# A four-layer attention kernel whose weights are split into f16 pairs at fixed powers of two, with the column maxima moved into the guard

## The chip, the cores and the metric

The kernel runs on one core of one Trainium2 chip. The metric is the device time of one execution in microseconds, here the median of three runs. Beside it stands one profiled execution, from which every duration is read.

## What is computed

The reference applies four layers to x of 2048 rows and 512 columns in f32. Layers 0 and 2 attend over a sliding window of 256 positions with the weights A; layers 1 and 3 attend over all 2048 positions with the weights B. There are 32 heads of 16 columns.

```python
def layer(x, wqkv, wo, window):
    h = layernorm(x)                            # eps 1e-5, no gain
    q, k, v = split_heads(h @ wqkv)             # 32 heads of 16
    s = (q @ k.T) * 16 ** -0.5                  # window: 0 <= i - j < 256, else -1e9
    return x + (softmax(s) @ v) @ wo

x = A_x                                         # B_x is not used
for _ in range(2):
    x = layer(x, A_wqkv, A_wo, True)
    x = layer(x, B_wqkv, B_wo, False)
```

The entries of x and of all weights are drawn from a normal distribution with a spread of 0.05.

## The kernel before

There are two paths. The fast path computes everything and also a flag, `okay`, which is good when all softmax sums lie in a safe range. A general path follows under a condition and runs only where the flag isn't good.

The fast path works on chunks of 512 rows (four chunks, `c`) and on groups of four heads (eight groups, `qd`). Chunks are normalised (`stats`, `norm`), transposed by DMA into `xc` and projected by `keys`, `queries` and `values`; `wo` is the output projection (`wo_part` in layer 3), and `epilogue` divides by the softmax sums. `exps` makes scores on PE (L724) and their exponentials on ACT (L728), which `attn_win` masks on POOL (L791, L794); the sums of products with V are L801 in window layers and L768 in full ones.

A projection is exact enough through f16 pairs: a weight matrix is split into a high and a low f16 part, x too, and three of the four products are added up in PSUM (`TERMS`). For the split the columns are first scaled by powers of two taken from the column maxima. This is the preparation of a matrix: `load_w` loads the raw f32 matrix (1 MB), `maxima` reduces absolute maxima on DVE (L295) and finishes them with four transposes on PE (L300), `scales` makes the powers of two and broadcasts them over all partitions by f32 matmuls (L328), and `parts` scales the matrix (L345, on POOL for the five matrices that are prepared during layer 0), casts the high part on ACT (L346), subtracts for the low part on POOL (L347) and writes the pair to DRAM (`wd`), from which the projections load it again. The scales are undone at the evictions of the projections (`es`, L534, L536, L537) and in the output projections (`gcol`, L662 and L683, followed by an addition to x, L663 and L684).

In the opening, before layer 0's attention, chunk 0 is projected from the raw weights by f32 matmuls with a transposed f32 x (`xT`); the maxima of these three matrices are made by transposing them on PE (`first_maxima`, L310). The pairs of these matrices are made at the end of the opening and used from chunk 1 on.

The order on PE is written out by the program: a planner (`Side`) puts pieces of projections between the steps of the attention, by costs and due times on a clock of its own. Works marked `aside` (normalisation, transposes, preparation) get their pieces at every step. The order on the other engines and on the one DMA queue, SP, is made by the scheduler from the dependencies and its own estimate of times; an instruction of low priority is taken where an earlier one isn't ready yet. All transfers are issued in order on SP, so one that waits holds those behind it.

At the end of each window layer stands a tail: the output projection of chunk 3, its normalisation and the projections that need it, before the next layer can begin (the calls of `tails`). Full layers use a single PSUM bank, `acc[1]`, for all side work.

Of the kernel before, what the change touches and what calls it, by code (L numbers as in the profile page):

```python
# [36 lines left out]
L_SUM = 2.0 ** 60  # L37

# [149 lines left out]
def fast_path(ctx, tc, flag, a_x, a_wqkv, a_wo, b_wqkv, b_wo, out):  # L188
# [21 lines left out]
    CM, DN, DC, WT, ST, pend = {}, {}, {}, {}, {}, []  # L210
# [16 lines left out]
    perm = cp.tile([P, P], F32, name="perm")  # L227
    onesf = cp.tile([P, P], F32, name="onesf")
    ones = cp.tile([P, QC], F16, name="ones")
    hsum = cp.tile([P, 32], BF16, name="hsum")  # L230
    es = cp.tile([P, 2, 2, NHT], F32, name="es")
    upv = cp.tile([P, 2, NHT], F32, name="upv")
    gcol = [cp.tile([P, D], F32, name=f"gcol{i}") for i in range(2)]
# [12 lines left out]
    nc.gpsimd.tensor_copy(perm.rearrange("p (h u d) -> p u h d", u=2, d=DH), ident.rearrange("p (u h d) -> p u h d", u=2, d=DH))  # L246
# [38 lines left out]
    def maxima(ty, s, raw):  # L285

        n = f"{ty}_{s}"
        if s == 3:
            for k in range(NC):
                nc.vector.tensor_scalar(raw[:, k, :], raw[:, k, :], upv[:, ty, k:k + 1], None, op0=ALU.mult)  # L290
        cm = CM[ty, s] = vp.tile([P, NHT], F32, name=f"wc{n}", tag="wc", bufs=8)
        am = vp.tile([P, D], F32, name=f"wa{n}", tag="dn", bufs=2)
        for h in range(4):
# [3 lines left out]
            yield  # L297
        pt = bank().rearrange("p (t f) -> p t f", f=P)
        for t in range(NHT):
            nc.tensor.transpose(pt[:, t, :], am[:, t * P:(t + 1) * P], ident)  # L300
        nc.vector.tensor_reduce(cm, pt, axis=AX.X, op=ALU.max)

    def first_maxima(s, raw, tiles):

        if (0, s) not in CM:
            CM[0, s] = vp.tile([P, NHT], F32, name=f"wc0_{s}", tag="wc", bufs=8)
        for t in tiles:
            pt = bank()
            for k in range(NC):
                nc.tensor.transpose(pt[:, k * P:(k + 1) * P], raw[:, k, t * P:(t + 1) * P], ident)  # L310
            nc.vector.tensor_reduce(CM[0, s][:, t:t + 1], pt, axis=AX.X, op=ALU.max, apply_absolute_value=True)

    def scales(ty, s):

        n = f"{ty}_{s}"
        cm = CM.pop((ty, s))
        up = es[:, ty, s, :] if s < 2 else vp.tile([P, NHT], F32, name=f"wu{n}", tag="wc", bufs=8)
        dn = vp.tile([P, NHT], F32, name=f"wn{n}", tag="wc", bufs=8)
        nc.vector.tensor_scalar(up.bitcast(I32), cm.bitcast(I32), 0x7F800000, None, op0=ALU.bitwise_and)
        nc.vector.tensor_scalar(dn.bitcast(I32), up.bitcast(I32), -1, 0x7F000000, op0=ALU.mult, op1=ALU.add)  # L320
        DC[ty, s] = dn
        for v, name in ((up, "u"), (dn, "d"))[0 if s == 3 else 1:]:
            dg = vp.tile([P, NHT, P], F32, name=f"{name}g{n}", tag="oe")
            nc.vector.tensor_tensor(dg, ident[:, None, :].broadcast_to([P, NHT, P]),
                                    v[:, :, None].broadcast_to([P, NHT, P]), ALU.mult)
            yield
            pb = bank()
            nc.tensor.matmul(pb, onesf, dg.rearrange("p t f -> p (t f)"), start=True, stop=True)  # L328
            if name == "u":
                nc.vector.tensor_copy(gcol[ty], pb)  # L330
            else:
                DN[ty, s] = vp.tile([P, D], F32, name=f"wd{n}", tag="dn", bufs=2)
                nc.scalar.activation(DN[ty, s], pb, AF.Copy)
        if s == 2:
            yield
            pu = bank()
            nc.tensor.matmul(pu[:, :NHT], perm, up, start=True, stop=True)
            nc.vector.tensor_copy(upv[:, ty, :], pu[:, :NHT])

    def parts(ty, s, raw, act):  # L340

        dnb = DN.pop((ty, s))
        w = wp.tile([P, NC, 2, D], F16, name=f"w{ty}_{s}", tag="vf", bufs=NQ)
        hi, lo = w[:, :, 0, :], w[:, :, 1, :]
        mul = lambda k: (nc.vector if act else nc.gpsimd).tensor_tensor(raw[:, k, :], raw[:, k, :], dnb, ALU.mult)  # L345
        cast = lambda k: nc.scalar.activation(hi[:, k, :], raw[:, k, :], AF.Copy)  # L346
        rest = lambda k: nc.gpsimd.tensor_tensor(lo[:, k, :], raw[:, k, :], hi[:, k, :], ALU.subtract)  # L347
        if act:
            for k in range(NC):
                mul(k), cast(k), rest(k)  # L350
                yield
            WT[ty, s] = w
# [869 lines left out]
```

## Time and the profile before

| What | us |
|---|---|
| median of three runs | 2755.56 (2751.47 to 2759.08) |
| profiled execution, its own time | 2751.01 |
| its span | 2749.2 |
| first scores of layer 0 | 64.12 |
| first scores of layer 1 | 499.95 |
| last addition to x | ends at 2742.19 |

The page gives busy time by engine, and views of the trace give the same by stage. PE's busy time is modelled to the end of each matmul, and matmuls overlap. The chain of waits follows the work back from the last instruction.

### The profile page before, as it was taken

The numbers are of one execution on the slowest core, as the hardware profiler recorded it, in microseconds if no ns is written. First come the engines' busy times: TensorE is split into PE (matmuls) and PEld (weight loads), VectorE is DVE, ScalarE is ACT, GpSimd is POOL, SyncE is SP. The second block draws the span as 40 slices with busy tenths as digits, with TensorE's granted clock in tenths as the row PEclk, the third lists the DMA queues.
The fourth block names the chain that finished last, engine by engine and source line by source line (L and its number), as shares of the span: only waits on it lengthen the run. The fifth ranks groups of instructions, "written<-read, shape, count | busy, mean of one in ns | idle before, by whom it ended". The sixth has DMA issues, their size and how long they took to land.

```text
span 2749.2 us, 59656 instructions
## 1 busy us (share of the span) xinstructions
PE 2632.0 (96%) x24358; PEld 772.6 (28%) x24358; DVE 955.6 (35%) x2059; ACT 2380.7 (87%) x2687; POOL 570.4 (21%) x1129
## 2 busy tenths in 40 slices
PE   8889999999999999999999989899999999999997
PEld 4333344322222222222223333522222222222221
DVE  7678765112131113112216467411222222222222
ACT  3566664799999999999997667499999999999997
POOL 2477672000000000000006678100000000000000
PEclk9999999999999999999999999999999999999999
DMA  6877676322232123212325556622334443333321
GB/s 214 231 248 228 197 228 191 117 70 90 86 100 87 61 85 108 82 64 91 99 72 151 173 152 173 181 75 93 112 111 126 123 117 105 99 111 114 99 95 56
DMA packets 318269, 344.78 MB, mean 125 GB/s; under 512 B 114080, under 2 KB 234144, under 8 KB 311968
## 3 DMA queue, kind: packets, MB, share of 16 engines
q1 hardware_dynamic: 317984, 340.86, 41.1%
q8 instruction: 193, 3.16, 0.5%
q14 instruction: 92, 0.75, 0.1%
HBM read 228.07 MB, written 96.99 MB: 118 GB/s over the span
## 4 chain that ended last, share of the span: by engine, by line
PE 74%; DVE 8%; ACT 7%; issue 4%; DMA 3%; POOL 2%; SPq 1%; ACTq 0%; DVEq 0%; POOLq 0%
PE acc L768 31%; PE s L724 19%; PE acc L435 10%; PE b L438 9%; ACT e L728 7%; PE acc L801 4%; PE bs L438 1%; DVE ot L696 1%; DVE sp L537 1%; POOL wr L345 1%; DVE xh L477 1%; DMA qt<-qs 1%; DVE xn L471 1%; DVE xh L471 1%; POOL e L791 0%
## 5 line engine op out<-in xcount | busy, mean ns | idle before, releaser
L728 ACT ACTIVATE e<-s 128x1024 f32<-128x1024 f32 (+2 forms) x2432 | 2246.5, 1114 | 122.4 <-PE s L724 107.3
L768 PE MATMUL acc<-e,vt 128*17 128x512 f32 x8192 | 1080.8, 599 | 5.2 <-DVE ot L696 4.2
L724 PE MATMUL s<-qt,kt 64*128 64x512 f16 (+3 forms) x5504 | 772.3, 355 | 52.4 <-ACT e L728 26.6
L724 PEld LDWEIGHTS <-kt 64*128 64x128 f16 x5504 | 199.6, 94 | 798.7 <-issue 765.9
L794 POOL TENSOR_SCALAR_AFFINE_SELECT e<-e 128x256 f32<-128x256 f32 x512 | 229.8, 457 | 106.6 <-ACT e L728 106.3
L768 PEld LDWEIGHTS acc<-e,vt 128*17 128x17 f32 x8192 | 136.3, 95 | 385.4 <-issue 353.1
L696 DVE STREAM_TRANSPOSE ot<-acc 128x512 f32<-128x512 f32 x128 | 91.4, 714 | 410.5 <-PE acc L768 320.7
L791 POOL TENSOR_SCALAR_AFFINE_SELECT e<-e 128x256 f32<-128x256 f32 x448 | 203.0, 459 | 81.7 <-ACT e L728 77.9
L712 POOL TENSOR_TENSOR oh<-o,oh 128x512 f16<-128x512 f32 x31 | 36.0, 1162 | 881.4 <-DVE oh L711 881.4
L801 PE MATMUL acc<-e,vt 128*17 128x384 f32 (+2 forms) x2816 | 202.1, 393 | 4.1 <-POOL e L791 4.0
L438 PE MATMUL b<-xc,w 128*128 128x512 f16 x672 | 159.6, 385 | 11.9 <-DVE sp L537 7.8
L542 POOL TENSOR_TENSOR sq_h<-sp_h 128x512 bf16<-128x512 f16 x27 | 28.1, 1041 | 486.3 <-DVE sp_h L536 486.3
L536 DVE TENSOR_SCALAR sp<-acc,es 128x512 f16<-128x512 f32 x28 | 20.9, 747 | 288.9 <-PE acc L435 277.1
L536 DVE TENSOR_SCALAR sp_h<-acc,es 128x512 f16<-128x512 f32 x27 | 20.3, 750 | 283.4 <-PE acc L435 283.3
L542 POOL TENSOR_TENSOR sq<-sp 128x512 bf16<-128x512 f16 x28 | 29.1, 1041 | 396.8 <-DVE sp L536 396.8
L648 DVE COPY vt<-acc 128x256 f32<-128x256 f32 (+1 forms) x36 | 18.5, 514 | 265.5 <-PE acc L435 265.5
L435 PE MATMUL acc<-xc,w_h 128*32 128x512 f16 x1296 | 108.5, 379 | 2.3 <-DVE km L575 2.3
L435 PE MATMUL acc<-xc,w 128*32 128x512 f16 x1344 | 108.9, 379 | 0.3
L683 DVE TENSOR_TENSOR dx<-acc,gcol 128x512 f32<-128x512 f32 x60 | 41.5, 692 | 176.6 <-PE acc L435 176.6
L435 PE MATMUL acc<-wo,oh 128*32 128x512 f16 x1296 | 101.4, 379 | 0.0
L534 ACT ACTIVATE sp<-b,es 128x512 f16<-128x512 f32 x56 | 38.5, 687 | 71.1 <-PE b L438 71.0
L438 PEld LDWEIGHTS <-w 128*128 128x128 f16 x720 | 66.5, 99 | 110.2 <-issue 42.2
(172 smaller groups left out, 1807.2 us busy)
## 6 DMA issues: line engine op xcount, KB each, us to landing
kt<-kf SPq DMA_DIRECT2D x128, 512.0 KB
qt<-qs SPq DMA_DIRECT2D x128, 256.0 KB
xd<-x SPq DMA_DIRECT2D x96, 256.0 KB
x<-xd SPq DMA_DIRECT2D x96, 256.0 KB
w<-wd SPq DMA_DIRECT2D x20, 1024.0 KB
kt<-kw SPq DMA_DIRECT2D x64, 256.0 KB
qs<-sp SPq DMA_DIRECT2D x48, 256.0 KB
wo<-wd SPq DMA_DIRECT2D x12, 1024.0 KB
```

The source lines that it names most:

```text
L435: nc.tensor.matmul(ps[g:g + 32], a[:, g:g + 32], b, start=(i == 0), stop=(i == len(pairs) - 1), skip_group_check=True)
L438: nc.tensor.matmul(ps, a, b, start=(i == 0), stop=(i == len(pairs) - 1))
L471: norm1 = lambda o: nc.vector.tensor_scalar(o, xs[i], mv[:, i, 0:1], y[:, i:i + 1], op0=ALU.subtract, op1=ALU.mult)
L542: nc.gpsimd.tensor_tensor(sq, sp[:, 0], sp[:, 0], ALU.mult)
L683: nc.vector.tensor_tensor(d, ps, gcol[1], ALU.mult)
L696: nc.vector.transpose(ot.rearrange("p b r -> p (b r)"), a)
L724: nc.tensor.matmul(ps[:, h, s0:s0 + wd_], kt[R * h:R * h + R, pr, kc:kc + P], qt[R * h:R * h + R, pr, qc:qc + wd_], start=True, stop=True)
L728: nc.scalar.activation(e[:, :, w0:w1], ps[:, :, w0:w1], AF.Exp, scale=SCALE)
L768: nc.tensor.matmul(a[32 * h:32 * h + DH + 1, :], V[l, qd // 4, j // 8][:, j % 8, 4 * (qd % 4) + h, :], es_[h // 2][:, h % 2, :], start=(j ...
L791: nc.gpsimd.affine_select(v, v, pattern=[[0, 2], [-1, P]], compare_op=ALU.is_gt, fill=0.0, base=0, channel_multiplier=1)
L794: nc.gpsimd.affine_select(v, v, pattern=[[0, 2], [1, P]], compare_op=ALU.is_ge, fill=0.0, base=0, channel_multiplier=-1)
L801: nc.tensor.matmul(a[32 * h:32 * h + DH + 1, q * P:(q + nb) * P], V[l, (4 * c + j) // 4][:, j % 4, 4 * qd + h, :], es_[h // 2][:, h % 2, s ...
```

## The change

Every matrix is split at one fixed power of two (2^7, for V's matrix 2^5) in place of a power per column. The preparation is then a load, a cast with a scale on ACT and one operation on DVE that scales and subtracts, four of each for a matrix. The maxima, scales, broadcasts and the scaling on POOL are gone. Chunk 0 is projected from the split weights with a split x, with the product of the high parts of all four tiles first. Query, key and value matrices of type A stay in SBUF for chunks 0 and 1. The output projections use one DVE operation with a constant instead of a product with `gcol` and an addition.

The guard is extended: `column_maxima` loads each of the eight raw matrices again, in the buffers of the window layers' V, and reduces it on DVE in four pieces; these works are put beside the first half of layer 1's chunk 0. `column_range`, in layer 2, checks that all column maxima lie between 2^-8 and 3.9, and the flag includes that.

```diff
+UP = {0: 2.0 ** 7, 1: 2.0 ** 7, 2: 2.0 ** 5, 3: 2.0 ** 7}
+C_MIN, C_MAX = 2.0 ** -8, 3.9
...
-    def load_w(ty, s):
-        raw = wp.tile([P, NC, D], F32, name=f"wr{ty}_{s}", tag="vf", bufs=NQ)
+    def load_w(ty, s, tag="vf", n="wr"):
+        raw = wp.tile([P, NC, D], F32, name=f"{n}{ty}_{s}", tag=tag, bufs=VB if tag == "vw" else NQ)
...
-    def maxima(ty, s, raw):
-    def first_maxima(s, raw, tiles):
-    def scales(ty, s):
-    def parts(ty, s, raw, act):
...
+    def parts(ty, s, raw):
+        w = wp.tile([P, NC, 2, D], F16, name=f"w{ty}_{s}", tag="vf", bufs=NQ)
+        for k in range(NC):
+            nc.scalar.activation(w[:, k, 0, :], raw[:, k, :], AF.Copy, scale=UP[s])
+            nc.vector.scalar_tensor_tensor(w[:, k, 1, :], raw[:, k, :], UP[s], w[:, k, 0, :], op0=ALU.mult, op1=ALU.subtract)
+            yield
+        nc.sync.dma_start(wd[ty, s], w)
+        if ty == 0 and s < 3:
+            WT[ty, s] = [w, w]
+
+    def prep(ty, s):
+        raw = load_w(ty, s)
+        yield wait(14)
+        for _ in parts(ty, s, raw):
+            yield wait(1.8)
+
+    def column_maxima(ty, s):
+        raw = load_w(ty, s, "vw", "wq")
+        yield wait(14)
+        am = vp.tile([P, D], F32, name=f"wa{ty}_{s}", tag="am", bufs=1)
         for h in range(4):
             f = slice(h * P, (h + 1) * P)
             nc.vector.tensor_reduce(am[:, f], raw[:, :, f].rearrange("p k f -> p f k"), axis=AX.X, op=ALU.max,
                                     apply_absolute_value=True)
+            yield wait(2)
+        at = vp.tile([P, D // 32, 32], F32, name=f"wb{ty}_{s}", tag="at", bufs=1)
+        nc.vector.transpose(at.rearrange("p b r -> p (b r)"), am)
+        yield wait(1)
+        nc.vector.tensor_reduce(cmax[:, ty, s, :], at, axis=AX.X, op=ALU.max)
+        yield wait(1)
+
+    def column_range():
+        pt = bank()
+        nc.tensor.transpose(pt[:, :P], cmax.rearrange("p t s b -> p (t s b)"), ident)
+        cols = vp.tile([P, 32], F32, name="cols", tag="cols", bufs=1)
+        nc.vector.tensor_reduce(cols, pt[:, :P].rearrange("p (a r) -> p r a", r=32), axis=AX.X, op=ALU.max)
+        nc.vector.tensor_reduce(okay[:, 2:3], cols, axis=AX.X, op=ALU.min)
+        nc.vector.tensor_reduce(okay[:, 3:4], cols, axis=AX.X, op=ALU.max)
...
+        if first:
+            for t in range(NHT):
+                begun.append(bank())
+                for k in range(NC):
+                    nc.tensor.matmul(begun[t], w[:, k, 0, t * P:(t + 1) * P], xc[:, 0, k, :], start=(k == 0), stop=False)
...
-            e = first[2][:, t:t + 1] if first else es[:, ty, s, t:t + 1]
+            e = 1.0 / UP[s]
...
-                nc.vector.tensor_tensor(d, ps, gcol[l % 2], ALU.mult)
-            nc.vector.tensor_add(xs[i], xs[i], d)
+                nc.vector.scalar_tensor_tensor(xs[i], ps, 1.0 / (UP[2] * UP[3]), xs[i], op0=ALU.mult, op1=ALU.add)
...
-            nc.vector.tensor_tensor(d, ps, gcol[1], ALU.mult)
-            (nc.gpsimd if last and i % 2 == 0 else nc.vector).tensor_tensor(xs[i], xs[i], d, ALU.add)
+            nc.vector.scalar_tensor_tensor(xs[i], ps, 1.0 / (UP[2] * UP[3]), xs[i], op0=ALU.mult, op1=ALU.add)
...
-    xT = wp.tile([P, NC, QC], F32, name="xT", tag="xc", bufs=NQ)
-    first_maxima(1, raw[1], (0, 1))
+    xT = XC[0, 0] = wp.tile([P, 2, NC, QC], F16, name="xc0_0", tag="xc", bufs=NQ)
+    raw = {m: load_w(0, m, "xc") for m in (1, 0, 2)}
...
-        nc.scalar.activation(xT[:, :, i * P:(i + 1) * P], pt, AF.Copy)
+        xh, xl = (xT[:, b, :, i * P:(i + 1) * P] for b in range(2))
+        nc.scalar.activation(xh, pt, AF.Copy)
+        nc.vector.tensor_tensor(xl, pt, xh, ALU.subtract)
+    run(parts(0, 1, raw[1]))
+    run(keys(0, 0, True, None, True))
+    run(parts(0, 0, raw[0]))
+    run(queries(0, 0, True))
+    run(parts(0, 2, raw[2]))
+    vals = values(0, 0, True)
+    next(vals), next(vals), next(vals)
     settle()
...
+            return [Work(column_range(), 0.0, None, [("C", *m) for m in mats], aside=True), OO(1, 3), Q(2, 2), T(2, 3)]
...
+    for i, m in enumerate(mats):
+        works[1][0].append(CM(*m, [("C", *list(mats)[i - 2])] if i > 1 else []))
...
+    nc.vector.tensor_mul(okay[:, 0:1], okay[:, 0:1], okay[:, 2:3])
```

More of the change, by code (lines that the diff above doesn't have):

```diff
@@ L313, in scales @@
-    def scales(ty, s):
[L315 to L338, printed above, removed]
@@ L437, in mms @@
             else:
[L438 removed]
+                nc.tensor.matmul(ps, a, b, start=(go and i == 0), stop=(i == len(pairs) - 1))
             spent(us)
@@ L611, in key_shift, with values @@
                               m[32 * t:32 * t + 8, None, :].broadcast_to([8, NT, P]))
-    def values(l, c, act, first=None, halves=(0, 1), tiles=range(4)):
+    def values(l, c, act, halves=(0, 1), tiles=range(4)):
         n = f"{l}_{c}_{halves[0]}_{tiles[0]}"
         HH, D0, D1 = H // 2, halves[0] * D // 2, (halves[-1] + 1) * D // 2
-        if not first:
-            w = weights(l % 2, 2, f"v{n}", D0, D1)
-            yield wait(8)
-            xc = XC[l, c]
+        here = (l % 2, 2) in WT
+        w = weights(l % 2, 2, f"v{n}", D0, D1)
+        yield wait(0 if here else 8)
+        xc = XC[l, c]
         dst = {}
```

159 lines of the change are left out of this document (33 added, 126 removed).

## The prediction

> **What bounds the kernel now.** I read the page's busy times first, then the busy time by stage, then the chain of waits inside the stage that the change touches most; the order of instructions of the built program, which holds no times, tells where the moved work now stands. The page shows PE and ACT as the two loaded engines, but as an average over stages with different limits:
>
> ```profile
> PE 2632.0 (96%) x24358; PEld 772.6 (28%) x24358; DVE 955.6 (35%) x2059; ACT 2380.7 (87%) x2687; POOL 570.4 (21%) x1129
> ```
>
> ```profile
> 0.00:64.00 64.00, 54.64 (x176) 28.87 (x176) 48.61 (x117) 20.73 (x33) 14.09 (x24) 1.00 0.65 207
> 64.00:440.00 376.00, 342.88 (x2981) 138.92 (x2984) 260.31 (x529) 241.78 (x317) 251.56 (x527) 0.99 0.76 225
> 440.00:504.00 64.00, 58.09 (x340) 29.29 (x336) 27.70 (x59) 22.39 (x40) 1.91 (x6) 0.98 0.68 209
> 504.00:1452.00 948.00, 938.40 (x9184) 221.80 (x9186) 183.82 (x425) 942.94 (x1020) 47.55 (x46) 1.00 0.27 82
> 1452.00:1782.00 330.00, 300.14 (x2933) 125.42 (x2925) 207.16 (x474) 212.22 (x261) 206.92 (x483) 0.97 0.60 173
> 1782.00:2750.00 968.00, 937.82 (x8761) 228.34 (x8757) 228.04 (x456) 940.61 (x1020) 48.41 (x44) 0.99 0.33 102
> ```
>
> The next view splits that. Its columns are stage, length, then busy time of PE, PEld, DVE, ACT and POOL, the granted clock, the DMA share and GB/s. The rows are the opening, layer 0, its tail, layer 1, layer 2 with its tail, and layer 3. Layers 1 and 3 are bound by ACT (942.94 of 948): the change takes no ACT work out of them, so they can lose but hardly gain. Whatever comes back must come out of the first 504 us. There PE is busy 342.88 of 376, so layer 0 yields its PE work that disappears and part of 33 us of gaps. The chain through 64 to 440 says what fills them:
>
> ```profile
> by line: PE b L438 32.0%; PE acc L801 12.9%; PE s L724 6.0%; POOL wr L345 5.1%; issue 3.4%; ACT e L728 2.9%; DMA kt<-kw 2.7%; POOL e L791 2.5%; POOL e L794 2.0%; DVE xn L471 1.9%; DVE xh L477 1.8%; DVE st L457 1.7%; DVE xh L471 1.7%; DMA x<
> ```
>
> POOL's scaling of weights (L345) carries 5.1% of 376, 19 us, more than the masks (L791, L794) that queue behind it.
>
> **The opening: -12.** Two pieces of the chain that are DMAs (the load of 1 MB of raw weights, and a transposed write of x), then the timeline of the opening:
>
> ```profile
> 2.68 6.35 DMA wr<-in_A_wqkv_dram
> 1759.61 3.29 DMA xc<-xh
> ```
>
> ```profile
> 9.16 1.09 PE L310 MATMUL bs<-ident,wr 128*128 128x128 f32 x4 [9.16 <-DMA wr<-in_A_wqkv_dram]
> 9.47 1.91 DVE L1081 TENSOR_SCALAR x<-x,mv,y 128x512 f32<-128x512 f32 x4
> 14.29 0.60 ACT L1085 ACTIVATE xT<-b 128x512 f32<-128x512 f32 x1
> 17.07 3.70 PE L438 MATMUL bs<-xT,wr 128*128 128x512 f32 x8 [0.20 <-DVE wc L311]
> 43.22 0.66 DVE L457 BATCH_NORM_STATS2 st<-x 128x6 f32<-128x512 f32 x1
> 52.93 4.06 SPq L498 DMA_TRANSPOSE xc<-xh  x3
> 55.51 0.74 DVE L591 TENSOR_SCALAR m_None<-b,kx 128x512 f16<-128x512 f32 x1
> 64.12 0.50 PE L724 MATMUL s<-qt,kt 64*128 64x384 f16 x4
> 72.57 2.76 PE L438 MATMUL b<-xc,w 128*128 128x512 f16 x12
> ```
>
> Before, twelve f32 tiles at some 3.5 us make K, Q and V of chunk 0, with 12 groups of L310 transposes ahead. Now 144 f16 matmuls do it, 2.76 us for 12, nearer 2.6 in a row: 12 x 2.6 = 31 us. The first weights land at 9.16; then ACT has 4 casts of weights and 4 of x, 8 x 0.6 = 5 us, so PE starts near 14 and ends near 46. DVE, by the order, has 15 splits of x and of weights ahead of the first eviction; at 0.75 (row L537 below) that is 11.2 us after 11.4, so 22.6, in time for the fifth tile, which needs the first tile's bank near 25. The query squares come after 10 of 12 tiles, at 41; from the mask row's start (55.51) to the first scores (64.12) was 8.6, so scores start near 50, 14 earlier. What is late next is chunk 1: its x loads now stand on SP behind the queries' writes, so its statistics end near 45. They ended at 43.88 before and the last transpose was issued by 56.99; 13.1 later plus 3.29 to land gives 61. K of chunk 1 started at 72.57, so 12 remain. Bounds: 16 (x in time) and 9.
>
> **Layer 0: -15.** Groups of instructions between 64 and 440 us (count, busy time, mean ns of one, idle time before), and below them two rows of the waits between 130 and 440:
>
> ```profile
> L537 DVE SCALAR_TENSOR_TENSOR sp<-b,es,sp 128x512 f16<-128x512 f32 x40 | 29.6, 745 | 54.1 <-ACT sp L534 46.0 <-DMA kf<-sp 4.5 <-DMA kt<-kw 3.5
> L347 POOL TENSOR_TENSOR w<-wr,w 128x512 f16<-128x512 f32 x24 | 29.5, 1251 | 1.5 <-ACT w L346 1.5
> L345 POOL TENSOR_TENSOR wr<-wr,wd 128x512 f32<-128x512 f32 x20 | 27.4, 1396 | 1.1 <-ACT wd L333 1.0
> L696 DVE STREAM_TRANSPOSE ot<-acc 128x512 f32<-128x512 f32 x31 | 22.0, 711 | 22.0 <-PE acc L801 21.2
> L295 DVE TENSOR_REDUCE wa<-wr 128x128 f32<-128x512 f32 x20 | 20.3, 1067 | 2.5 <-DMA wr<-in_B_wqkv_dram 2.4
> L663 DVE TENSOR_TENSOR x<-x,dx 128x512 f32<-128x512 f32 x12 | 8.8, 737 | 0.3
> L346 ACT ACTIVATE w<-wr 128x512 f16<-128x512 f32 x24 | 14.5, 634 | 11.9 <-POOL wr L345 8.5 <-DVE wr L345 3.4
> L328 PE MATMUL b<-dg,onesf 128*128 128x512 f32 x10 | 5.6, 645 | 1.8 <-DVE dg L324 1.8
> L328 PE MATMUL b<-ug,onesf 128*128 128x512 f32 x4 | 2.2, 644 | 0.0
> L300 PE MATMUL b<-ident,wa 128*128 128x128 f32 x20 | 3.3, 287 | 0.0
> ```
>
> ```profile
> PEld acc L801 <- POOL e L791: 9.9, 18, 1.8
> PE acc L801 <- POOL e L791: 3.7, 5, 1.4
> ```
>
> The scale broadcasts (L328) and the transposes of maxima (L300) go: PE loses 5.6 + 2.2 + 3.3 = 11 us, which counts in full where PE is busy nine tenths. POOL loses 29.5 + 27.4 = 57; PE's waits for masks are 9.9 + 3.7 = 13.6, and I credit under half, 6, because a mask also waits for its exp. ACT keeps its 20 casts (0.634 each), but in fours: 2 us for exps held behind 2.5 us. DVE trades 20 reductions for 20 splits of 0.75. Together -15. Bounds: -5 (ACT lumps and DVE collisions eat the rest), -26 (11, 13.6 and some scaling stalls).
>
> A split reads two SBUF tensors while POOL masks. An old DVE op of that kind (two SBUF inputs) ran beside POOL in the opening, by the timeline:
>
> ```profile
> 36.91 5.86 POOL L347 TENSOR_TENSOR w<-wr,w 128x512 f16<-128x512 f32 x4 [33.26 <-ACT w L346]
> 39.00 1.64 DVE L345 TENSOR_TENSOR wr<-wr,wd 128x512 f32<-128x512 f32 x1
> ```
>
> It took 1.64. 20 splits at 1.64 instead of 0.75 add 18 us of DVE time; with half of that on PE's evictions, layer 0 gains 6, not 15. I take 0.75, since a mask is far shorter than POOL's weight ops. The Trainium skill, GPSIMD Engine Reference, section Specifications, says the same against this change: POOL's SBUF interface is shared with VectorE and collides with its instructions that read two SBUF inputs; by that rule the layer gains 6, and the row just shown agrees.
>
> **The column maxima: +3, +6, +1.** The diff puts them beside layer 1, but the order of instructions in the built program has seven of eight matrices' reductions on DVE ahead of layer 1: three within chunk 3, one at its end, three in the tail between the layers; only the last stands inside layer 1. In chunk 3 that is 12 x 1.067 + 3 x 0.71 = 15 us of DVE, in gaps while PE works; the second and third load wait on SP for the reductions before, with query and key loads behind: +3 (0 to 12). The tail's timeline:
>
> ```profile
> 457.80 0.32 SPq L399 DMA_DIRECT2D w<-wd  x1
> 460.20 0.17 DVE L43 TENSOR_SCALAR v<-mv 128x4 f32<-128x4 f32 x1
> 462.58 0.16 DVE L466 SCALAR_TENSOR_TENSOR nb<-mv,y 128x4 f32<-128x4 f32 x1
> 474.96 2.75 PE L438 MATMUL b<-xc,w 128*128 128x512 f16 x12 [1.09 <-DMA xc<-xh]
> ```
>
> The tail has no slack: DVE's steps from 460.20 to 462.58 lead to xc, for which PE already waits 1.09. Four reductions and a transpose now stand among those steps, 4 x 1.067 + 0.71 = 5.0 us; the query weights' load (457.80) falls behind the last x write and two column loads: +6 (0 to 13). Nothing covers either, so this is the term whose bound I trust least. In layer 1 the last matrix's four reductions wait for their load and hold an eviction of the values behind them; PE runs two or three exps ahead there, so of 5 us I take +1 (0 to 5).
>
> **The rest: -4.** One DVE op replaces product and addition (0.737 each) in the output projections. In layer 2 three stand on the chain, -2.2, and the range check (one transpose, six DVE ops) gives back 1; its tail -0.7. In layer 3 ACT hides them: 0. At the end,
>
> ```profile
> 2738.06 0.81 PE L438 MATMUL b<-wo,oh 128*128 128x512 f16 x3
> 2741.50 0.69 DVE L684 TENSOR_TENSOR x<-x,dx 128x512 f32<-128x512 f32 x1
> ```
>
> the last addition ended at 2742.19, 3.3 after PE; one op of 0.75 now follows: -2.
>
> Sum: -12 - 15 + 3 + 6 + 1 - 1.2 - 0.7 - 2 = -21, against the profiled execution's 2751.01. The median of the three runs lies 4.55 above it; I carry the difference over: 2755.56 - 21 = 2735.
>
> **Rivals.** First, slower: SP becomes the bound. A column load (6.35) and its four reductions (4.3) take 10.6 us, and the next load holds SP for it: two in chunk 3, 21 us, of which one group of heads (376/32 = 12 us) is hidden: +9. In the tail 4 MB more at 209/0.68 = 307 GB/s are 14 us, with 5 on DVE: +19. Layer 1 +5. If POOL's relief is lost too, -12 - 11 - 4 + 33 = +6, and with chunk 3's full 12 +9: 2765. It decides from a tail of about 85 us instead of 64. For it: DMA share already 0.76 and 0.68. Against: loads were placed where DMA had room in the order. Second, no change: the early start is given back because chunk 1 is not ready before 72; layer 0 keeps PE's 11: -11 + 10 - 4 = -5, 2750. Third, the port collisions above: 2744. Fourth, the change doesn't do what it says: columns fall outside the guard's bounds and the general path runs; weights drawn at 0.05 leave column maxima near 0.15, so 0.01.
>
> **Numbers.** Forecast 0.60, rival one 0.18, two 0.13, three 0.08, four 0.01. 0.3% is 8 us, about what a measurement can tell. Faster 0.68, same 0.13, slower 0.19. All low bounds give -49 (2707), the slow rival 2765; I keep 2710 to 2765, which leaves out about 2 in 10.
>
> **What would show it.** Right: first scores near 50, K of chunk 1 near 61, layer 0 around 360 us, the tail near 70, layer 1 still 948. Wrong: scores near 64; PE waiting on kt or qt loads in chunk 3; a tail over 80; POOL masks still ahead of PE.

## The result and the profile after

The changed kernel takes 2727.72 us (median of four runs, 2724.67 to 2732.27) against 2753.51 for the kernel before beside it: a ratio of 0.9906 with a 95% interval of 0.9883 to 0.9930. That is 25.8 us less, where 21 were forecast. In a second set it took 2729.35 (five runs, ratio 0.9914, 0.9901 to 0.9928). The total fits the forecast; its terms do not all.

Line numbers shift: L438, L724, L768, L801 and L593 of the kernel before are L376, L658, L702, L735 and L537 of the changed one. The experiments shift them a little further; names of tiles stay.

The page's busy times of the changed kernel:

```profile
PE 2605.4 (95%) x24315; PEld 757.2 (28%) x24315; DVE 849.5 (31%) x1933; ACT 2371.7 (87%) x2683; POOL 495.6 (18%) x1074
```

Busy time by stage (stage, length, then PE, PEld, DVE, ACT, POOL, granted clock, DMA share, GB/s):

```profile
0.00:47.50 47.50, 36.06 (x170) 17.39 (x171) 30.04 (x76) 21.92 (x37) 2.66 (x15) 1.00 0.79 283
47.50:432.40 384.90, 338.00 (x2965) 135.95 (x2966) 224.47 (x505) 233.11 (x309) 198.49 (x485) 0.96 0.81 232
432.40:496.00 63.60, 56.49 (x300) 28.46 (x298) 42.68 (x79) 17.91 (x35) 0.65 (x2) 0.92 0.72 221
496.00:1450.00 954.00, 943.30 (x9244) 223.85 (x9244) 178.06 (x420) 947.70 (x1026) 48.06 (x47) 1.00 0.28 85
1450.00:1765.00 315.00, 292.54 (x2882) 123.20 (x2882) 191.58 (x459) 209.94 (x258) 200.32 (x483) 0.99 0.63 179
1765.00:2730.00 965.00, 939.00 (x8766) 228.37 (x8765) 182.69 (x395) 941.13 (x1021) 45.47 (x42) 0.99 0.33 102
```

POOL's work in layer 0 fell by 53 us and DVE's by 36, as the diff says, yet the layer is not shorter. Its granted clock fell from 0.99 to 0.96, and in the tail from 0.98 to 0.92. The stages of all kernels, read from their timelines (us; "K" is the first matmul of the keys of chunk 1; a layer runs from its first scores, layer 2 from the end of layer 1, layer 3 from its first sum with V, to its last sum with V; the two tails lie between the layers, and "end" is what follows layer 3; "half" is time at half clock within layer 0, added up from the trace's clock record):

| kernel | first scores | K | layer 0 | half | tail | layer 1 | layer 2 | its tail | layer 3 | end | profiled execution | median |
|---|---|---|---|---|---|---|---|---|---|---|---|---|
| before | 64.1 | 72.6 | 377.9 | 10 | 57.9 | 955.7 | 274.8 | 50.9 | 950.0 | 17.9 | 2751.0 | 2753.5 |
| changed | 47.5 | 57.9 | 384.9 | 31 | 63.8 | 954.1 | 263.6 | 51.1 | 950.1 | 15.4 | 2732.3 | 2727.7 |
| changed, again | 49.8 | 58.9 | 380.5 | 34 | 63.5 | 954.1 | 263.6 | 50.9 | 948.7 | 15.3 | 2728.2 | 2729.4 |
| no maxima | 48.2 | 58.5 | 377.4 | 38 | 56.9 | 955.5 | 271.0 | 52.4 | 948.7 | 16.1 | 2727.9 | 2727.1 |
| range check only | 48.5 | 58.7 | 375.9 | 34 | 57.3 | 954.7 | 265.7 | 49.8 | 949.0 | 14.3 | 2716.9 | 2718.9 |
| maxima held | 48.0 | 58.2 | 379.6 | 38 | 57.6 | 961.6 | 265.4 | 53.4 | 950.1 | 15.6 | 2732.9 | 2731.1 |
| x early | 55.5 | 60.7 | 377.5 | 25 | 63.5 | 954.1 | 261.6 | 48.2 | 948.7 | 15.6 | 2726.4 | 2727.9 |
| two operations | 49.3 | 59.7 | 386.9 | 41 | 65.9 | 955.2 | 266.4 | 50.0 | 949.0 | 17.3 | 2741.8 | 2747.1 |
| own buffer | 48.9 | 59.0 | 388.9 | 31 | 65.7 | 955.3 | 264.8 | 53.6 | 949.9 | 17.9 | 2746.8 | 2747.1 |
| two in full layers | 49.5 | 60.0 | 385.3 | 41 | 63.6 | 954.2 | 263.4 | 50.4 | 948.9 | 18.0 | 2735.0 | 2734.1 |
| before, one operation | 64.5 | 72.9 | 376.0 | 10 | 55.3 | 954.6 | 271.1 | 51.2 | 949.7 | 15.7 | 2740.0 | 2740.1 |
| no casts | 48.3 | 58.6 | 385.5 | 34 | 63.3 | 954.4 | 263.6 | 53.2 | 950.3 | 15.7 | 2736.1 | 2732.4 |
| maxima late | 48.9 | 59.1 | 374.4 | 34 | 56.6 | 959.5 | 265.6 | 53.9 | 949.7 | 15.5 | 2725.8 | 2724.9 |
| all late | 48.6 | 58.7 | 366.5 | 24 | 55.9 | 954.0 | 267.2 | 50.8 | 948.7 | 15.5 | 2708.9 | 2708.7 |

The opening, by the timeline of PE, matches the forecast; what follows it was not in the sum:

```profile
47.49 0.50 PE L658 MATMUL s<-qt,kt 64*128 64x384 f16 x4 [0.45 <-DMA qt<-qs]
50.73 1.29 PE L735 MATMUL acc<-e,vt 128*17 128x384 f32 x8
57.91 5.05 PE L376 MATMUL b<-xc,w 128*128 128x512 f16 x12 [5.88 <-DMA xc<-xh]
```

The twelve matmuls that took 2.76 us before take 5.05 here. Short stretches of the same by-stage view say why (the third number from the end is the granted clock):

```profile
47.50:52.00 4.50, 3.05 (x24) 0.94 (x24) 4.46 (x9) 4.31 (x7) 3.25 (x6) 1.00 0.81 221
52.00:55.80 3.80, 0.02 (x2) 0.00 (x0) 2.36 (x4) 0.29 (x1) 3.80 (x7) 1.00 0.77 142
55.80:62.60 6.80, 4.69 (x12) 1.61 (x12) 2.52 (x6) 0.00 (x0) 0.01 (x1) 0.50 0.96 245
62.60:69.40 6.80, 6.80 (x53) 2.52 (x52) 5.63 (x19) 4.61 (x8) 2.79 (x6) 1.00 0.58 197
```

PE stood still, and 3.8 us into the pause its clock was halved for 6.8 us, the first 4.7 of work included. Such a pause costs twice; not every pause does (the one at 183.9 us left the clock at full, and the last section shows why). In layer 0 of the kernel before there were two pauses over 2 us, 5.1 us together, and 10 us at half clock; in the changed one seven, 25.7 us, and 31 us. What makes them is in the waits of PE in layer 0 (us in total, times, longest):

```profile
PE s L658 <- ACT e L662: 21.5, 28, 3.0
PE b L376 <- DMA xc<-xh: 5.9, 1, 5.9
PE s L658 <- DMA kt<-kw: 4.8, 1, 4.8
PE acc L735 <- POOL e L725: 4.4, 2, 3.9
PE b L376 <- DVE sp L481: 3.3, 1, 3.3
```

and behind three of these waits, in the timeline of all engines between 182 and 212 us:

```profile
182.93 2.19 ACT L288 ACTIVATE w<-wr 128x512 f16<-128x512 f32 x4 [2.42 <-DMA wr<-in_B_wqkv_dram]
...
186.93 0.61 PE L658 MATMUL s<-qt,kt 64*128 64x128 f16 x8 [3.03 <-ACT e L662]
...
200.89 2.17 ACT L288 ACTIVATE w<-wr 128x512 f16<-128x512 f32 x4
...
204.02 0.39 PE L658 MATMUL s<-qt,kt 64*128 64x256 f16 x4 [2.72 <-ACT e L662]
...
208.23 2.49 DVE L289 SCALAR_TENSOR_TENSOR w<-wr,w 128x512 f16<-128x512 f32 x4
...
210.78 0.33 POOL L571 MEMSET vt<- 128x128 f32 x1 [11.06 <-DVE w L289]
210.96 0.41 POOL L725 TENSOR_SCALAR_AFFINE_SELECT e<-e 128x256 f32<-128x256 f32 x1
...
211.42 0.62 PE L735 MATMUL acc<-e,vt 128*17 128x128 f32 x4 [3.94 <-POOL e L725]
```

Four casts of one matrix stand ahead of the exponentials and first wait 2.42 for their load: PE waits 3.03. The next four wait for nothing, but take 2.17 together: PE waits 2.72. Their four splits begin 5 us after the casts have ended; POOL is to fill a buffer of V that the raw matrix still holds, waits 11.06 for the splits, and the masks wait behind it on POOL: PE waits 3.94. From 206.0 to 216.2 the clock is at half.

The tail shows what was forecast for the column maxima (timeline):

```profile
456.43 1.01 DVE L308 TENSOR_REDUCE wa<-wq 128x128 f32<-128x512 f32 x1
...
460.13 5.30 PE L376 MATMUL b<-xc,w 128*128 128x512 f16 x12 [4.51 <-DMA w<-wd]
462.98 0.16 DVE L404 SCALAR_TENSOR_TENSOR nb<-mv,y 128x4 f32<-128x4 f32 x1
```

Reductions stand among the steps that lead to nb, and the weights' load, behind the column loads on SP, holds PE for 4.51.

### The profile page after: what moved, and what is told of

Same layout as the page of the kernel before. It is cut to its first block, busy times and chain, and to the rows that moved or that the text cites. A ratio compares the mean times of both kernels' runs of the same rounds, so it can differ in the third digit from the quotient of the medians.

```text
span 2730.5 us, 59360 instructions
## 1 busy us (share of the span) xinstructions
PE 2605.4 (95%) x24315; PEld 757.2 (28%) x24315; DVE 849.5 (31%) x1933; ACT 2371.7 (87%) x2683; POOL 495.6 (18%) x1074
## 4 chain that ended last, share of the span: by engine, by line
PE 75%; ACT 8%; DVE 7%; issue 4%; DMA 4%; SPq 1%; POOL 1%; ACTq 0%; DVEq 0%
PE acc L702 31%; PE s L658 20%; PE acc L373 10%; PE b L376 9%; ACT e L662 7%; PE acc L735 4%; PE bs L376 1%; DVE ot L630 1%; DVE wa L308 1%; DVE xh L415 1%; DMA wr<-in_B_wqkv_dram 1%; DMA wq<-in_A_wqkv_dram 1%; DVE xn L409 1%; DMA kt<-kw 0%; DMA kt<-kf 0%
## 5 line engine op out<-in xcount | busy, mean ns | idle before, releaser
L702 PE MATMUL acc<-e,vt 128*17 128x512 f32 x8192 | 1080.4, 599 | 5.1 <-DVE ot L630 4.1
L658 PE MATMUL s<-qt,kt 64*128 64x512 f16 (+3 forms) x5504 | 773.6, 356 | 57.0 <-ACT e L662 30.5
L658 PEld LDWEIGHTS <-kt 64*128 64x128 f16 x5504 | 199.9, 94 | 802.5 <-issue 769.8
L728 POOL TENSOR_SCALAR_AFFINE_SELECT e<-e 128x256 f32<-128x256 f32 x512 | 229.4, 455 | 176.5 <-ACT e L662 175.9
L702 PEld LDWEIGHTS acc<-e,vt 128*17 128x17 f32 x8192 | 136.3, 95 | 385.7 <-issue 353.5
L725 POOL TENSOR_SCALAR_AFFINE_SELECT e<-e 128x256 f32<-128x256 f32 x448 | 197.4, 446 | 104.5 <-ACT e L662 100.8
L735 PE MATMUL acc<-e,vt 128*17 128x384 f32 (+2 forms) x2816 | 197.9, 392 | 4.5 <-POOL e L725 4.4
L376 PE MATMUL b<-xc,w 128*128 128x512 f16 x700 | 172.0, 395 | 15.0 <-DMA xc<-xh 5.9
L478 ACT ACTIVATE sp<-b 128x512 f16<-128x512 f32 x59 | 35.3, 598 | 89.3 <-PE b L376 85.8
L376 PEld LDWEIGHTS <-w 128*128 128x128 f16 x800 | 74.8, 100 | 128.9 <-issue 49.4
L480 DVE TENSOR_SCALAR sp<-acc 128x512 f16<-128x512 f32 x28 | 19.3, 689 | 290.7 <-PE acc L373 278.5
L480 DVE TENSOR_SCALAR sp_h<-acc 128x512 f16<-128x512 f32 x27 | 18.6, 690 | 285.2 <-PE acc L373 285.2
L618 DVE SCALAR_TENSOR_TENSOR x<-acc,x 128x512 f32<-128x512 f32 x60 | 41.5, 692 | 206.1 <-PE acc L373 199.6
L376 PE MATMUL b<-wo,oh 128*128 128x512 f16 x390 | 95.3, 382 | 6.0 <-DVE x L600 3.2
```

The costliest lines, as they stand in the source:

```text
L376: nc.tensor.matmul(ps, a, b, start=(go and i == 0), stop=(i == len(pairs) - 1))
L480: nc.vector.tensor_scalar(sp[:, 0], ps, e, None, op0=ALU.mult)
L618: nc.vector.scalar_tensor_tensor(xs[i], ps, 1.0 / (UP[2] * UP[3]), xs[i], op0=ALU.mult, op1=ALU.add)
L658: nc.tensor.matmul(ps[:, h, s0:s0 + wd_], kt[R * h:R * h + R, pr, kc:kc + P], qt[R * h:R * h + R, pr, qc:qc + wd_], start=True, stop=True)
L702: nc.tensor.matmul(a[32 * h:32 * h + DH + 1, :], V[l, qd // 4, j // 8][:, j % 8, 4 * (qd % 4) + h, :], es_[h // 2][:, h % 2, :], start=(j ...
L725: nc.gpsimd.affine_select(v, v, pattern=[[0, 2], [-1, P]], compare_op=ALU.is_gt, fill=0.0, base=0, channel_multiplier=1)
```

## The experiments

**1. No column maxima** (and without the factor in the flag)

```diff
-            return [Work(column_range(), 0.0, None, [("C", *m) for m in mats], aside=True), OO(1, 3), Q(2, 2), T(2, 3)]
+            return [OO(1, 3), Q(2, 2), T(2, 3)]
...
-    for i, m in enumerate(mats):
-        works[1][0].append(CM(*m, [("C", *list(mats)[i - 2])] if i > 1 else []))
...
-    nc.vector.tensor_mul(okay[:, 0:1], okay[:, 0:1], okay[:, 2:3])
```

> This kernel leaves out the column maxima, their second loads of the eight matrices and their factor in the flag, so the guard does not look at the columns. Theory (the column work stands in order on DVE and SP at places where PE has no slack): the tail of layer 0 falls from 63.8 us to about 58, the waits of DVE in chunk 3 for the column loads (6.1 us in the changed kernel) and of PE for kt and qt behind them go, layer 0 shortens by 4 to 8, the whole by 10 to 14 us, to about 2716. Rival (the column work is hidden and the tail became longer for another reason, such as the clock): the tail stays within 2 us of 63.8 and the whole within 4 us of the changed kernel's 2727.7.

2727.09 us (ratio 0.9906, 0.9891 to 0.9921): no gain. Yet the tail took 56.9 and layer 0 377.4, both as the theory has it: 14 us less. Half of that came back in layer 2 (271.0 instead of 263.6), and some 3 in layer 1 and layer 2's tail; the 4 us that the profiled execution is still shorter don't show in the medians.

**2. Range check only**

```diff
+    nc.vector.memset(cmax, 1.0)
...
-            return [Work(column_range(), 0.0, None, [("C", *m) for m in mats], aside=True), OO(1, 3), Q(2, 2), T(2, 3)]
+            return [Work(column_range(), 0.0, None, aside=True), OO(1, 3), Q(2, 2), T(2, 3)]
...
-    for i, m in enumerate(mats):
-        works[1][0].append(CM(*m, [("C", *list(mats)[i - 2])] if i > 1 else []))
```

> The changed kernel without the column loads and reductions, but with the range check of layer 2 kept, on maxima set to 1 (so the guard looks at no columns). Theory (the kernel without maxima gained 14 us in layer 0 and its tail and lost them in layer 2, because without the range check the writes of the mask rows in layer 2's second chunk came to stand ahead of key loads on SP): here those writes stand as in the changed kernel, layer 2 takes 264 us, layer 0 about 378, the tail 57, and the whole is 8 to 12 us below the changed kernel's 2728. Rival (the time comes back somewhere whatever is taken out, since other waits are there): within 4 us of 2728, with layer 2 near 271 again.

2718.93 us (0.9880, 0.9861 to 0.9898), 9 us below the changed kernel, with layer 2 at 265.7: the sizes are the theory's. Its mechanism is not what the timelines show, though. PE in the second chunk of layer 2, without maxima and range check:

```profile
1495.63 0.70 PE L658 MATMUL s<-qt,kt 64*128 64x384 f16 x8
1496.26 1.06 PE L735 MATMUL acc<-e,vt 128*17 128x128 f32 x16
1502.63 1.04 PE L658 MATMUL s<-qt,kt 64*128 64x128 f16 x8 [5.32 <-DMA qt<-qs]
```

in the changed kernel:

```profile
1511.55 0.61 PE L658 MATMUL s<-qt,kt 64*128 64x384 f16 x8
1512.09 1.06 PE L735 MATMUL acc<-e,vt 128*17 128x128 f32 x16
1513.08 1.90 PE L376 MATMUL b<-xc,w 128*128 128x512 f16 x8
1514.92 0.61 PE L658 MATMUL s<-qt,kt 64*128 64x128 f16 x8
```

and in this experiment:

```profile
1493.32 0.61 PE L659 MATMUL s<-qt,kt 64*128 64x128 f16 x8 [2.60 <-DMA qt<-qs]
```

In the changed kernel a piece of a projection (L376) stands between the steps of the attention, and the query load lands meanwhile. Without the range check PE has no projection at that place and waits 5.32; the kernel before waits there too, 4.08. So by these timelines the planner's order on PE, which one more work in its list moved, is a part of what made layer 2 shorter. With the range check alone PE still waits 2.60, so this wait explains about half of the 5.3 us between the two experiments; the order of loads on SP differs as well, and no run moved one without the other.

**3. Maxima held back to layer 1**

```diff
-    def load_w(ty, s, tag="vf", n="wr"):
+    def load_w(ty, s, tag="vf", n="wr", held=False):
...
+        if held:
+            nc.vector.tensor_copy(raw[:, :, 0:1], lsum[:, None, 0:1].broadcast_to([P, NC, 1]))
...
-        raw = load_w(ty, s, "vw", "wq")
+        raw = load_w(ty, s, "vw", "wq", True)
...
-        works[1][0].append(CM(*m, [("C", *list(mats)[i - 2])] if i > 1 else []))
+        works[1][1].append(CM(*m, [("C", *list(mats)[i - 2])] if i > 1 else []))
```

> The column loads cannot start before the output projections that stand ahead of them in layer 1, so that all eight matrices' reductions stand inside layer 1, where ACT sets the pace. Theory (the place costs, not the work): tail of layer 0 near 58 us, layer 0 shorter by 4 to 8, layer 1 no more than 2 us longer, the whole 8 to 14 us below the changed kernel. Rival (the work costs the same wherever it stands, since its DVE pieces hold evictions of the single bank that full layers use for side work): what tail and layer 0 gain, layer 1 loses, by 6 to 12 us, and the whole stays within 4 us.

2731.13 us (0.9920, 0.9907 to 0.9934). The tail fell to 57.6, but layer 1 grew to 961.6: the rival. What the reductions (L310 there) waited for, in us and times:

```profile
  DMA wq<-in_A_wqkv_dram: 10.8, 2
  DMA wq<-in_B_wqkv_dram: 10.5, 2
```

DVE stood 21 us at the head of its queue for loads that had not landed.

**4. Maxima late** (experiment 3 with this edit on top)

```diff
-        yield wait(14)
+        yield wait(40)
         am = vp.tile([P, D], F32, name=f"wa{ty}_{s}", tag="am", bufs=1)
+        nc.vector.tensor_copy(am[:, ::P], lsum[:, 0:1].broadcast_to([P, 4]))
```

> A candidate. Column loads cannot start before layer 1, and each matrix's reductions begin some 40 us after its load (one small copy from the latest epilogue holds them). Theory (in layer 1 it was DVE waiting for a load, 21 us in four waits, that held evictions of the single bank and made layer 1 longer by 7.5 us, not the reductions): layer 1 is back at 954 to 956 us, the tail 57, layer 0 380, the whole 2720 to 2724. Rival (the reductions themselves hold the evictions): layer 1 stays near 961 and the whole near 2730.

2724.91 us (0.9897, 0.9881 to 0.9912). The waits for loads are gone, but layer 1 stays at 959.5: each theory has half. What is left stands behind two matrices' reductions in a row (timelines of DVE and PE, the second matrix's):

```profile
729.22 3.94 DVE L311 TENSOR_REDUCE wa<-wq 128x128 f32<-128x512 f32 x4
...
733.82 0.65 DVE L534 TENSOR_SCALAR m_None<-acc 128x512 f16<-128x512 f32 x1
...
734.53 0.87 PE L376 MATMUL acc<-wo,oh 128*32 128x512 f16 x12 [2.87 <-DVE m_None L534]
```

The eviction L534 waits for them, PE for the eviction, and ACT then stands idle for 3.1 and 1.1 us, 4 of the 5.4 that layer 1 is longer.

**5. x early**

```diff
-            xs = load_x(0, c)
+            xs = early.pop() if c == 1 else load_x(0, c)
...
+    early = []
...
+    early.append(load_x(0, 1))
     run(parts(0, 1, raw[1]))
```

> The loads of x for chunk 1 are issued ahead of the first weights' pairs instead of behind the queries' writes. Theory (after the first scores PE is short of work until chunk 1 is ready, and the granted clock falls behind that pause): K of chunk 1 starts near 53 us instead of 57.9, its first twelve matmuls take nearer 2.8 than 5.05 us, and layer 0 ends some 5 us earlier. Rival (layer 0 is paced by later waits for loads, so an earlier start is given back): K of chunk 1 starts earlier but the last PV of layer 0 stays within 2 us of 432.4. Second rival: the transposes now stand ahead of the query loads on SP and the first scores move back by 3 us or more.

2727.86 us (0.9922, 0.9908 to 0.9937), no difference. The second rival holds: the transposes came ahead of the query loads, first scores moved back from 47.5 to 55.5, and K started at 60.7. Layer 0 ended at 433.0, as in the changed kernel (432.4). K did not start earlier here, so whether layer 0 would keep an earlier start stays open.

**6. Two operations again**

```diff
-                nc.vector.scalar_tensor_tensor(xs[i], ps, 1.0 / (UP[2] * UP[3]), xs[i], op0=ALU.mult, op1=ALU.add)
+                nc.vector.tensor_scalar(d, ps, 1.0 / (UP[2] * UP[3]), None, op0=ALU.mult)
+            nc.vector.tensor_add(xs[i], xs[i], d)
...
```

> The output projections again use two operations on DVE (a product with a constant, then an addition), all else as in the changed kernel. Theory A (the single operation is what shortened layer 2 by 11.2 us): layer 2 takes about 273 us instead of 263.6, the end 2 us more, the whole 9 to 14 us longer. Theory B (what I forecast: 2 to 3 us of chain in layer 2, 0.7 in its tail, 2 at the end; the rest of the 11.2 came from the order of loads on SP, from the clock, or from the spread of one execution): layer 2 within 3 us of 263.6 and the whole 4 to 6 us longer.

2747.14 us (0.9985, 0.9976 to 0.9994): 18 to 19 us longer, more than either theory. Layer 2 takes 266.4, so the single operation isn't what shortened it by 11. The cost is spread: 2 to 6 us in layer 0, 2 in the tail, 1 in layer 1, 3 in layer 2, 2 at the end. The profiled execution, 2741.8, lies below the median, so some 5 us stay without a place.

**7. The product in buffers of its own** (experiment 6 with this edit on top, in layer 3 alike)

```diff
-            d = vp.tile([P, D], F32, name=f"dx{l}_{c}_{i}", tag="xn", bufs=1)
+            d = vp.tile([P, D], F32, name=f"dx{l}_{c}_{i}", tag="dx", bufs=2)
```

> As the kernel with two operations (2747.1), but the product goes to two buffers of its own instead of the single buffer that it shared with the normalised rows (xn). Theory (the shared buffer costs: a product waits until the normalisation's cast has read it, and the other way round): the whole returns to within 6 us of the changed kernel. Rival (the operations themselves cost, by their time on DVE and their place in its order): still 12 us or more above the changed kernel.

2747.10 us (0.9975, 0.9963 to 0.9986): the rival. It isn't the shared buffer.

**8. Two operations in the full layers alone**

```diff
+            if l % 2:
...
+                    nc.vector.tensor_scalar(d, ps, 1.0 / (UP[2] * UP[3]), None, op0=ALU.mult)
+                nc.vector.tensor_add(xs[i], xs[i], d)
...
```

> Two operations only in the full layers' output projections (layers 1 and 3), one in the window layers. Theory (the cost sits in the window layers and their tails, which PE bounds with little slack; ACT hides it in the full ones): within 4 us of the changed kernel, of which 2 us at the end. Rival (the cost sits in the full layers, where DVE's eviction of the single bank holds PE): within 4 us of 2747.

2734.14 us (0.9927, 0.9914 to 0.9941): 4.8 us more than the changed kernel beside it (2729.35) and so just outside the theory's 4; the end has 2.6 of them (18.0 against 15.4). By subtraction the other 13 are the window layers' and their tails'; the stages of the two kernels with two operations everywhere place 7 to 10 of them there.

**9. The kernel before with one operation**

```diff
-                nc.vector.tensor_tensor(d, ps, gcol[l % 2], ALU.mult)
-            nc.vector.tensor_add(xs[i], xs[i], d)
+                nc.vector.scalar_tensor_tensor(xs[i], ps, 0.125, xs[i], op0=ALU.mult, op1=ALU.add)
...
```

> The kernel before, with the output projections by the one operation of DVE and a constant of 1/8 in place of the power per column (1/8 is the power that nearly all columns have), all else as it was. Theory A (the single operation is most of the change): some 15 to 20 us below the kernel before, near 2733. Theory B (its price is what I forecast, and putting two operations into the changed kernel hurt by something else, such as their place): 3 to 6 us below, near 2746.

2740.06 us (0.9953, 0.9940 to 0.9967), 12.7 below the kernel before, between the theories and nearer to A. The constant is not the columns' power, as the expectation has it (V's power is in it too), which alters values and not instructions. By stage: 1.9 in layer 0, 2.6 in the tail, 1.1 in layer 1, 3.7 in layer 2, 2.2 at the end.

**10. The changed kernel again**, with no edit

> The changed kernel itself once more, beside the three experiments below, for the spread of its stages from one profiled execution to the next. If the stages of a single execution can be trusted to 2 us, layer 0 again takes 385, the tail 64 and layer 2 about 264 us, with half-clock stretches after the same pauses of PE. If layer 2 comes back at 270 or more, its gain of 11.2 us was the luck of one execution.

Layer 2 came back at 263.6 and the tail at 63.5, layer 0 at 380.5 instead of 384.9. Six of its seven pauses are at the same places; the half-clock stretches at them differ (at the first, 13.7 us that begin 4.8 us ahead of the pause, in place of 6.8 that begin within it).

**11. No casts in layer 0**

```diff
-        for _ in parts(ty, s, raw):
-            yield wait(1.8)
+        yield wait(7.2)
+        for b in range(2):
+            nc.sync.dma_start(wd[ty, s][:, :, b, :], zeros[:, None, :].broadcast_to([P, NC, D]))
```

> The changed kernel with the casts on ACT and the splits on DVE left out for the five matrices prepared in layer 0; their loads and the writes of the pairs stay, but the pairs are zeros (so the output is not the reference's). Theory (casts and splits stand in order on ACT and DVE ahead of exponentials, wait for their loads, and so make the pauses of PE near 158, 185, 203 and 209 us, each followed by some 3 to 10 us at half clock): these pauses go, and layer 0 falls from 381 to 385 us to 365 to 370. Rival (the pauses come from loads of keys and queries behind the 5 MB on SP and the DMA engines): they stay, layer 0 within 4 us of 381.

2732.39 us (0.9927, 0.9914 to 0.9941), layer 0 385.5. The pauses at 158, 184 and 202 went, but a new one came at 180 (waits of PE in layer 0):

```profile
PE s L659 <- DMA kt<-kw: 15.5, 2, 11.1
```

The order on SP was another there: the eight pieces of B_wo's load stood ahead of the query and key loads. The time is about the rival's, and so is the kind of the new wait: a key load behind the loads of weights. It doesn't decide what made the old pauses.

**12. All late** (experiment 4 with this edit on top)

```diff
-        works[1][1].append(CM(*m, [("C", *list(mats)[i - 2])] if i > 1 else []))
+        works[1][1].append(CM(*m, [("C", *list(mats)[i - 1])] if i else []))
...
-        yield wait(14)
-        for _ in parts(ty, s, raw):
+        yield wait(45)
+        for _ in parts(ty, s, raw, True):
...
+            up = vp.tile([P, 1], F32, name=f"hu{ty}_{s}", tag="hu")
+            nc.vector.tensor_scalar(up, lsum[:, 0:1], 0.0, UP[s], op0=ALU.mult, op1=ALU.add)
-            nc.scalar.activation(w[:, k, 0, :], raw[:, k, :], AF.Copy, scale=UP[s])
+            nc.scalar.activation(w[:, k, 0, :], raw[:, k, :], AF.Copy, scale=up)
```

> A candidate on top of the one before it (2724.9): one matrix's reductions at a time (each load waits for the matrix before), and in layer 0 the casts of the five prepared matrices stand some 2 to 3 groups of heads after their loads instead of one, held by a scale that is computed behind the latest epilogue. Theory (casts and splits, which wait in order for loads or for each other, make the pauses of PE near 202 and 208 us and the half-clock stretch behind them): those pauses go and layer 0 falls from 374.4 to 365 to 370 us; with the pairs of reductions gone layer 1 falls from 959.5 to about 956; the whole about 2714 to 2720. Rival (the pauses belong to the bursts of transfers between the layers' pieces, whatever ACT and DVE do): layer 0 stays within 3 us of 374 and the pauses only move.

2708.74 us (four runs, 2708.56 to 2713.67), a ratio of 0.9853 with an interval of 0.9836 to 0.9869: 43.5 us below the kernel before and some 19 below the change, with the whole guard. Layer 0 took 366.5, layer 1 954.0, as the theory has it; the whole lies below the 2714 to 2720 that it gave. Busy time by stage (layer 0, its tail, layer 1):

```profile
48.60:415.10 366.50, 336.40 (x2965) 135.68 (x2966) 210.53 (x492) 234.47 (x309) 205.80 (x485) 0.97 0.82 232
415.10:471.00 55.90, 53.70 (x302) 27.96 (x300) 24.61 (x55) 18.11 (x36) 0.00 (x0) 1.00 0.69 206
471.00:1425.00 954.00, 943.38 (x9246) 223.74 (x9248) 213.97 (x478) 947.18 (x1024) 48.64 (x49) 1.00 0.30 92
```

and the waits of PE in layer 0:

```profile
PE s L665 <- ACT e L669: 17.7, 28, 1.0
PE b L383 <- DMA xc<-xh: 5.1, 1, 5.1
PE s L665 <- DMA kt<-kw: 4.7, 1, 4.7
PE acc L742 <- POOL e L732: 1.3, 2, 0.8
```

The work is the changed kernel's, piece for piece (PE 336.40 against 338.00). What is gone is the long waits: no exponential or mask holds PE for more than 1.0 us, where it was 3.0 and 3.9, and two pauses over 2 us are left of the changed kernel's seven. The transfers moved along with the casts: B_wo's load, issued from 181.5 to 185.9 us in experiment 4, is issued from 189.8 to 212.1 here. So the move as a whole is shown to pay; how much of it is the engines' queues and how much the transfers is not.

## Why the prediction was right or wrong

**The opening (-12): right.** First scores came at 47.5 and 49.8 (50 was forecast), K at 57.9 and 58.9 (61), so K came 13.7 to 14.7 earlier where 12 were forecast. What follows on an early start was not in the sum: PE was now ready 6 us before chunk 1, and this pause and its half-clock stretch are a part of the next term.

**Layer 0 (-15, and +3 for the reductions): wrong.** From K to its end the layer took 369.5 us before, 374.4 and 371.4 in the changed kernel: 2 to 5 more, where 12 less were forecast; from its first scores 385 and 380, where the prediction's own sign of being right was 360. Three terms failed.

The casts: "2 us for exps held behind 2.5 us" priced them once, by their own time. In the trace three of the seven pauses, 9.7 us together, hang on casts and splits: one on the casts' own time, one on it and a wait for their load, one on a buffer that the splits still read. The time at half clock, 31 us instead of 10, was not in the sum at all. Moving casts and splits later, with the transfers that go with them (experiment 12 against experiment 4), gave 374.4 - 366.5 = 7.9 us. That the waits in the queues made the loss, and not the order of the transfers, is argued from the waits that are gone; experiment 11 does not support it.

The reductions in chunk 3 were priced at +3 with a bound of 12. The two kernels without them took 377.4 and 375.9 against 384.9 and 380.5, so 3 to 9.

The masks: of the 13.6 us of waits for them 9.9 were those of weight loads, which overlap PE's work. PE's own waits for masks (3.7 before, between 130 and 440) are 4.4 in the changed kernel, nearly one event, and 1.3 in the last: POOL lost 53 us of work, but at most some 3 were to be had from it, not 6.

With casts and reductions out of the way the layer takes 356.4 us from K on, 13.1 less than before, of which the single operation has 1.9. So most of the -15 was there, and the changed kernel spent it on waits.

**The tail (+6): right.** 63.8 and 63.5 against 57.9, by reductions among DVE's steps and by the weights' load behind the column loads, both as told; 56.9 and 57.3 without them. What the forecast didn't have is that 10 us of the tail ran at half clock, around these waits; in the kernel before none of it did. Layer 1 (+1) showed nothing, 954.1 against 955.7.

**The rest (-4): far too small, and this hid the error in layer 0.** The single operation was given 2.2 us in layer 2, 0.7 in its tail and 2 at the end. Layer 2 (3.7) and the end (2.2) were near. But on the kernel before it is worth 12.7 us in all and in the changed one 18 to 19: the sum left out layer 0 (1.9 on the kernel before) and its tail (2.6), where the same chain stands, and layer 1 (1.1). Why it is worth more in the changed kernel stays open. The range check was priced at +1 and gave -5 to -7 in layer 2, by an accident: as one more work it moved the planner's order, in part to where a load had held PE. It explains most of layer 2's -11.2, with the single operation's 3.7.

So -21 against -25.8 is in good part luck, a sum of errors: from K on, layer 0 came out 14 to 17 us longer than forecast, layer 2 10 shorter, the opening and layer 1 2 to 3 shorter each. The profiled executions show -18.7 and -22.8, so 3 to 7 us of the -25.8 stand in no stage. (The bounds that the prediction calls all low add to -46, not -49; the range doesn't hang on it.)

**The rivals.** SP as the bound did not come: it decides from a tail of 85, which is 64. The early start was not given back as the second rival had it: chunk 1 was ready at 58, not 72, and layer 0 ended 10 to 12 us earlier; it lost elsewhere what it should have gained besides. Of the prediction's signs of being wrong one showed, masks still ahead of PE (4.4 us); waits for key or query loads in chunk 3 did not. The port collisions were there, but small. The 20 splits of layer 0 took

```profile
L289 DVE SCALAR_TENSOR_TENSOR w<-wr,w 128x512 f16<-128x512 f32 x20 | 13.7, 715 | 4.8 <-ACT w L288 4.8
```

0.715 us each in the mean (0.75 was taken), not 1.64. But most of them met no mask: the thirteen that ran with no POOL operation beside them took 0.68 to 0.69, and the four slowest, 0.80 to 0.89, ran beside two masks in a row, as this one:

```profile
139.87 0.81 DVE L289 SCALAR_TENSOR_TENSOR w<-wr,w 128x512 f16<-128x512 f32 x1
```

The Trainium skill's rule (GPSIMD Engine Reference, Specifications: POOL's SBUF interfaces are shared with VectorE and contend with its instructions that have two SBUF inputs) agrees with that. Beside masks, which took 0.4 us each, it cost up to 0.2 us a split, beside POOL's weight operations 1 us.

## What to carry to other kernels

An operation that is taken off an engine's total is worth little if what stays or comes new on another stands in order ahead of the critical stream: price what waits behind it, and look for buffers that tie engines together. Where a scheduler places work by its own estimate of transfers, a false dependency on a late event can hold it back; here such holds, for casts and for reductions, gave some 19 us beside the change's 26. And a kernel with one part undone can come out even because an order elsewhere moved, and a forecast can be right because its errors cancel: compare stage by stage before calling a part free.

## What the runs showed of the hardware

PE's granted clock is 1.00 or 0.50 in all fourteen profiled executions. Within one execution the stretches at 0.50 begin at times that lie whole multiples of 3.41 us apart, and last 3.4 us or a multiple, up to 13.7: the clock changes only on a grid of windows. Cut into these windows, PE's busy share (modelled, as the page says) tells what follows. Of all windows at full clock none busier than 0.62 was followed by half clock, and none less busy than 0.41 by full clock; from half clock it came back only behind a window of at least 0.82.

So what counts is how much of one window a pause takes, not its length. In the changed kernel a pause of 2.1 us (158.4 to 160.5) lay in one window and the clock was halved behind it; one of 3.0 us (183.9 to 186.9) was split between two and the clock stayed:

```profile
158.18:161.59 3.41, 1.31 (x18) 0.59 (x20) 3.20 (x8) 1.17 (x3) 0.71 (x2) 1.00 0.75 297
161.59:165.00 3.41, 3.41 (x21) 1.11 (x14) 0.80 (x3) 1.89 (x3) 2.21 (x6) 0.50 0.82 232
182.07:185.49 3.42, 1.83 (x26) 0.62 (x24) 1.90 (x4) 2.56 (x5) 0.00 (x0) 1.00 1.15 341
185.49:188.90 3.41, 1.97 (x26) 0.84 (x27) 2.01 (x4) 2.90 (x4) 2.80 (x7) 1.00 1.13 188
188.90:192.31 3.41, 3.41 (x27) 1.44 (x29) 1.01 (x2) 1.12 (x2) 2.01 (x6) 1.00 1.10 115
```

In the two executions of the changed kernel a window begins 1.5 and 0.3 us behind the first scores. So the grid isn't tied to the program, and the stretches at the same pauses differ. The Trainium skill (TensorE: Matmul & The Clock Gate, What's actually happening) has the clock halved after at least one idle window of about 3.4 us, with free-running windows. The trace agrees on the half and on the windows, but the window need not be idle: in the one from 158.18 us PE was busy for 1.31 of 3.41 us.

Over a whole execution the time at half clock was 49 us in the kernel before, 67 and 62 in the changed one and 49 in the last.
